# A written issue order for VectorE, ScalarE and GpSimd in the first 13 units of a fused attention, gated-FFN and FFT kernel

## The chip, the cores and the metric

The kernel runs on one core of a Trainium2 chip. The metric is device time in microseconds: the median of three runs. Besides, one execution was profiled; its span is the time from the first to the last instruction of the program.

## What is computed

Three layers in a row, all in float32, over 4 batches of 576 tokens (32 global, 512 local) and 512 features (8 heads of 64):

```python
# 1 attention: local tokens see a band of +-32 keys and the global ones; global tokens see all
s_l = concatenate([scale*q_l@k_g.T, where(|i-j|<=32, scale*q_l@k_l.T, -1e9)])
out = concatenate([sm(scale*q_g@k_all.T)@v_all, sm(s_l)@v_all])      # sm: e/(sum(e)+1e-9)
# 2 gated feed-forward with a convolution over tokens, d_ff = 1024
h = relu(x @ w_in)
c = conv_w[0]*h[t-1] + conv_w[1]*h[t] + conv_w[2]*h[t+1]
x = (h * sigmoid(c)) @ w_out
# 3 FFT mixing, layer norm and a feed-forward of 2048
u = x + real(fft(fft(x, tokens), features))
y = u + relu(norm(u) @ w_ch1) @ w_ch2
```

The weights arrive as 64-bit floats and are turned into float32 on the chip.

## The kernel before, in words

**Units.** The attention is cut into 32 units (`NU`; batch, half of the local tokens, pair of heads). For unit i, `load_qk` brings queries and keys, `s_mm` (called S below) makes four 128x224 score tiles on TensorE, `s_max` (M, L311) adds the mask and takes the row maximum on VectorE, `s_exp` (E, L323) does the exponentials on ScalarE, `s_norm` (L328 to L334) adds 1e-9 and inverts the sums on VectorE and scales the four tiles on GpSimd, `t_mm` (T) transposes them on TensorE, `t_evac` (L353) copies them out (VectorE one half, ScalarE the other), and `pv_mm` (V) multiplies by the values. `pv_evac` (L389, L390) splits the result into a high and a low part. The last two units of a half batch also run the global tokens (`sg_piece`, `pg_soft`, `pg_trans`, `pg_pv`).

**Feed-forward.** Layer 2 runs in 64 pieces u, two per unit from unit 6 on: `m_g1` (F, 12 matmuls and the ReLU, L479), `m_conv` (L489 to L491), `m_tanh` (L497), `m_gate` (L508 to L510) and three pieces later `m_g2` (D, 12 matmuls). Every operand of a matmul is a high and a low part (`mm3`: three products).

**Weights.** Layer 2 has 16 weight tiles of 128x512. For each, `fetch_w` loads 512 KB, and `make_w` makes the two float32 parts: absolute value on ScalarE (L167), clamp on GpSimd (L168), the low word's shift (ScalarE L170 for even tiles, VectorE L172 for odd ones), two joins of bits on VectorE (L174, L175), a copy to the high part on ScalarE (L203), and the low part on VectorE (L204). Two buffers `mag` hold the values in between. The list `wsteps` places the 16 in the program's units 0 to 8. Twelve of layer 3's tiles go the same way in units 11, 13, ..., 33 (`KEEP0`, `keep_make`), and are stored to DRAM for later.

**Order.** On SP (which issues the loads) and TensorE the instructions stand in the order in which the program writes them. On VectorE, ScalarE and GpSimd a list scheduler orders them, with a priority for each function (`PRIORITY`). On the chip each engine takes its instructions strictly in its order, each one waiting for its semaphores. After the attention come the FFT by matmuls, the layer norm and the last feed-forward, some 480 us of mostly TensorE work.

Of the kernel before, what the change touches and what calls it, by code (L numbers as in the profile page):

```python
# [38 lines left out]
MT = [(0, 92), (92, 92), (184, 90)]  # L39

# [88 lines left out]
def fused_kernel(ctx: ExitStack, tc: tile.TileContext, d, out):  # L129
# [172 lines left out]

    @prio("ev")
    def s_max(i):
        sb = s_bank.pop(i)
        sm = ap2.tile([128, 16], F32, tag="sm", name="sm", bufs=4)
        smalls[i] = sm
        for h in range(2):
            for a in range(2):
                k = 2 * h + a  # L310
                dve.tensor_tensor_reduce(  # L311
                    out=pbs(i)[h][:, a, 0:224], in0=sb[h][:, a], in1=mask[:, 2 * where(i)[1] + a], scale=-0.125,
                    scalar=3.0e38, op0=ALU.add, op1=ALU.min, accum_out=sm[:, k:k + 1],
                )
# [69 lines left out]
    def pv_evac(w):  # L384
        b, half, pp = where(2 * w)
        pvb = pv_bank.pop(w).rearrange("p (a q) -> p a q", a=2)
        t0 = SG + 256 * half
# [4 lines left out]
    smg_t = {}

    @prio("glo")
    def sg_piece(g, piece, tag):
# [5 lines left out]
        if piece == 0:  # L401
            smg_t[g] = ap2.tile([128, 8], F32, tag="smg", name="smg")
        sm = smg_t[g]
        with pri("ev"):
            dve.tensor_tensor_reduce(
                out=sg4s[g % 2][:, kc], in0=sb, in1=gmask[:, kc], scale=-0.125, scalar=3.0e38, op0=ALU.add,
                op1=ALU.min, accum_out=sm[:, piece:piece + 1],
            )
# [12 lines left out]

    @prio("glo")
    def pg_trans(g, tag, tag2):
        p = ap1.tile([128, 5, 128], F32, tag="pgt", name="pgt")
        t1, t2 = bank(tag), bank(tag2)
# [4 lines left out]
        with pri("ev"):  # L430
            act.copy(p[:, 0:4], t1.rearrange("p (s c) -> p s c", s=4))
            dve.tensor_copy(p[:, 4], t2[:, 0:128])
        pg_t[g] = p

    @prio("glo")
    def pg_pv(g, tag):
        b, gg = divmod(g, 2)
# [8 lines left out]
        xh, xl = get_xt(b)  # L446
        cs = slice(2 * gg, 2 * gg + 2)
        with pri("ev"):
            act.copy(xh[:, cs, 0:SG], o)
            dve.tensor_sub(xl[:, cs, 0:SG], o, f32(xh[:, cs, 0:SG]))  # L450
# [16 lines left out]
    def m_g1(u, tag):  # L467
# [10 lines left out]
        with pri("ev"):  # L478
            act.activation(hbuf[u % NHB][:, h0:h0 + n], o, AF.Relu, scale=0.5)  # L479

    @prio("me")
# [500 lines left out]
```

## Time and profile before

| | us |
|---|---|
| median of 3 runs (lowest, highest) | 799.74 (797.51, 800.78) |
| the profiled execution | 796.53 |
| its span | 794.6 |
| busy in the span: TensorE / VectorE / ScalarE / GpSimd | 765.2 / 477.9 / 365.1 / 159.2 |

The profiled execution is 3.2 us faster than the median of the runs; 1.9 us of its time lie outside its span. Busy time of TensorE counts a matmul at half the clock for twice as long, and a wait inside a group of matmuls can hide in it. In the rows of the views, a time in front of an instruction is its start from the beginning of the span, then comes its duration; brackets give the idle time of the engine before it and what ended it.

### The profile page before, as it was taken

The page shows a single profiled execution, that of the slowest core. Times are in us where ns is not written, and L with a number is a line of the kernel's source. Part 1 is how long each engine was busy: PE and PEld are TensorE (multiplying, and loading weights), DVE is VectorE, ACT ScalarE, POOL GpSimd, SP SyncE. Part 2 cuts the span into 40 slices and gives each one's busy share as a digit, 9 for nine tenths or more (in the row PEclk, how much of TensorE's full clock was granted, in tenths as well). Part 3 has the DMA queues.
Part 4 walks back from the last instruction along what each step waited for, and adds up shares of the span by engine and source line. Part 5 has one row for each costly group of instructions (what it writes and reads, how often), then busy time and mean ns, then how long its engine had stood idle before and what let it go on. Part 6 is the DMA issues. An engine that isn't in the chain of part 4 may idle for free.

```text
span 794.6 us, 13609 instructions
## 1 busy us (share of the span) xinstructions
PE 765.2 (96%) x5272; PEld 704.4 (89%) x5272; DVE 477.9 (60%) x1167; ACT 365.1 (46%) x884; POOL 159.2 (20%) x213
## 2 busy tenths in 40 slices
PE   6589999999999999999999999999999999999997
PEld 4368989998999988899889999999999999999997
DVE  6999787778777877699775778535422232213113
ACT  6787776777677775545533384313122112211110
POOL 5644423222322221000222022100022012100000
PEclk9889999999999999999999999999999999999999
DMA  8913423442345233436530670020200020001001
GB/s 310 401 45 108 141 79 126 135 168 79 127 134 169 78 111 107 115 114 234 182 102 1 225 254 1 1 91 0 66 26 2 1 90 1 1 1 45 1 1 45
DMA packets 36944, 77.80 MB, mean 98 GB/s; under 512 B 3768, under 2 KB 22072, under 8 KB 36880
## 3 DMA queue, kind: packets, MB, share of 16 engines
q1 hardware_dynamic: 36288, 74.52, 27.0%
q0 software_dynamic: 592, 2.42, 1.2%
q8 instruction: 41, 0.67, 0.3%
q14 instruction: 23, 0.19, 0.1%
HBM read 61.72 MB, written 15.20 MB: 97 GB/s over the span
## 4 chain that ended last, share of the span: by engine, by line
PE 85%; DVE 7%; DMA 3%; ACT 3%; issue 1%; POOL 1%; SPq 0%; DVEq 0%; POOLq 0%; ACTq 0%
PE ps_a L146 34%; PE ps_g L146 23%; PE ps_pv L146 15%; PE ps_s L146 6%; PE ps_t L146 3%; DMA qk<-in_qk_dram 2%; PE ps_s L344 1%; PE ps_t L344 1%; PE ps_s L345 1%; PE ps_t L345 1%; DMA uc<-u_d 1%; ACT pb L323 1%; DVE uc L857 1%; DVE cf L854 1%; DVE mag L174 1%
## 5 line engine op out<-in xcount | busy, mean ns | idle before, releaser
L146 PE MATMUL ps_a<-g,w_w 128*128 128x254 f32 (+1 forms) x768 | 112.7, 295 | 0.2 <-DVE u L541 0.2
L146 PE MATMUL ps_g<-x,w_w 128*128 128x256 f32 (+1 forms) x768 | 111.0, 293 | 1.1 <-ACT h L479 1.1
L146 PEld LDWEIGHTS ps_g<-x,w_w 128*128 128x128 f32 x768 | 100.3, 188 | 6.6 <-issue 4.4
L146 PEld LDWEIGHTS ps_a<-g,w_w 128*128 128x128 f32 x768 | 100.8, 190 | 4.5 <-issue 3.8
L146 PE MATMUL ps_a<-hd,w_w 128*128 128x436 f32 (+1 forms) x480 | 101.4, 360 | 0.0
L334 POOL TENSOR_SCALAR pb<-pb,sm 128x224 f32<-128x224 f32 x128 | 76.1, 613 | 109.2 <-DVE sm L329 42.3
L146 PEld LDWEIGHTS ps_a<-hd,w_w 128*128 128x128 f32 x480 | 90.1, 188 | 4.8
L826 DVE SCALAR_TENSOR_TENSOR hd<-ps_g,hd 128x436 fp32r<-128x436 f32 (+1 forms) x40 | 24.3, 608 | 88.7 <-ACT hd L825 88.7
L168 POOL TENSOR_SCALAR mag<-mag 128x512 f32<-128x512 f32 x48 | 39.6, 827 | 185.0 <-ACT mag L167 183.6
L146 PE MATMUL ps_a<-hd,w_v 128*128 128x436 f32 (+1 forms) x360 | 76.2, 360 | 0.0
L826 DVE SCALAR_TENSOR_TENSOR hd<-ps_pv,hd 128x436 fp32r<-128x436 f32 (+1 forms) x40 | 24.2, 605 | 85.1 <-ACT hd L825 85.1
L825 ACT ACTIVATE hd<-ps_pv 128x436 fp32r<-128x436 f32 (+1 forms) x40 | 21.3, 533 | 115.0 <-PE ps_pv L146 115.0
L825 ACT ACTIVATE hd<-ps_g 128x436 fp32r<-128x436 f32 (+1 forms) x40 | 21.3, 534 | 110.1 <-PE ps_g L146 110.0
L146 PEld LDWEIGHTS ps_a<-hd,w_v 128*128 128x128 f32 x360 | 67.6, 188 | 3.7
L323 ACT ACTIVATE pb<-pb,sm 128x224 f32<-128x224 f32 x128 | 60.4, 473 | 10.6 <-DVE sm L311 10.3
L490 DVE SCALAR_TENSOR_TENSOR y<-h,convw,y 128x254 f32<-128x254 f32 (+1 forms) x64 | 33.7, 527 | 29.0 <-ACT y L489 29.0
L146 PE MATMUL ps_g<-chl,w_w 128*128 128x436 f32 (+1 forms) x240 | 51.0, 361 | 0.0
L146 PE MATMUL ps_s<-qk 64*128 64x224 f32 (+1 forms) x144 | 38.3, 418 | 13.1 <-DMA qk<-in_qk_dram 8.0
L146 PE MATMUL ps_pv<-chl,w_v 128*128 128x436 f32 (+1 forms) x240 | 50.8, 360 | 0.0
L146 PE MATMUL ps_pv<-chl,w_w 128*128 128x436 f32 (+1 forms) x240 | 50.8, 360 | 0.0
L146 PEld LDWEIGHTS ps_pv<-chl,w_v 128*128 128x128 f32 x240 | 45.1, 188 | 2.5
L146 PEld LDWEIGHTS ps_g<-chl,w_w 128*128 128x128 f32 x240 | 44.8, 188 | 2.7 <-issue 0.3
(221 smaller groups left out, 1422.5 us busy)
## 6 DMA issues: line engine op xcount, KB each, us to landing
v<-in_v_dram SPq DMA_DIRECT2D x16, 640.0 KB, 4.9
qk<-in_qk_dram SPq DMA_DIRECT2D x16, 464.0 KB, 5.3
raw_r<-in_ch_dram SPq DMA_DIRECT2D x14, 512.0 KB, 6.2
raw_v<-in_ch_dram SPq DMA_DIRECT2D x13, 512.0 KB, 9.4
kept<-w_o SPq DMA_DIRECT2D x12, 512.0 KB, 3.8
w_w<-kept SPq DMA_DIRECT2D x12, 512.0 KB, 4.4
qk<-in_qk_dram SPq DMA_DIRECT2D x16, 304.0 KB, 4.9
u_d<-u SPq DMA_DIRECT2D x4, 1088.0 KB, 5.2
```

Source lines behind the costliest of these rows:

```text
L146: return pe.matmul(o, a, b, start=start, stop=stop)
L168: (clamp or dve).tensor_scalar(mag, mag, TOP, 2.0, op0=ALU.min, op1=ALU.max)
L174: dve.scalar_tensor_tensor(val, val, 3, tail, op0=ALU.logical_shift_left, op1=ALU.bitwise_or)
L323: last_exp[0] = act.activation(p, p, AF.Exp, bias=sm[:, k:k + 1], scale=-1.0, accum_out=sm[:, 4 + k:5 + k])
L334: gp.tensor_scalar(p, p, sm[:, k:k + 1], 1.0, op0=ALU.mult, op1=ALU.mult)
L344: pe.transpose(tb[:, 128 * a:128 * a + 128], pb[:, a, 0:128], ident)
L345: pe.transpose(tb[:, 256 + 128 * a:384 + 128 * a], pb[:, a, 128:256], ident)
L490: dve.scalar_tensor_tensor(y, hb[:, cc - 1:cc - 1 + n], convw2[:, m, 0:1], y, op0=ALU.mult, op1=ALU.add)
L825: act.activation(hd[:, 0], o, AF.Relu)
L826: dve.scalar_tensor_tensor(hd[:, 1], o, 0.0, f32(hd[:, 0]), op0=ALU.max, op1=ALU.subtract)
L854: dve.tensor_mul(tmp[:, e], acc[e], rs_t[c])
L857: dve.tensor_add(o, o, tmp[:, e])
```

## The change

The first 13 units (0 to 12) are no longer written as a loop. A table `PLAN` lists their steps one by one, each named by a short code and its indices, and inside it the order of VectorE, ScalarE and GpSimd is the written one too, not the scheduler's. The functions are split so that the table can place each instruction: `M3.0` is the first mask-and-maximum of unit 3, `E3.0` its exponential, `A3` and `R3` the sum plus 1e-9 and its inverse, `N3.0` a scaling, `T3.0` and `C3.0` transpose and copy-out, `XH`, `XL` the split of an attention result, `F5` and `D5.0` the feed-forward matmuls, `Y`, `TH`, `B` convolution, tanh and gate. `lw4` loads the fourth weight tile, and `wa wc wt/wu ws wo wh wl` are its seven steps (`wt` the shift on ScalarE, `wu` on VectorE). From unit 13 on the loop runs as before.

Besides the order: `A` runs on ScalarE where VectorE had L328 (13 times, and twice `GA` where it had L416); 10 of 16 shifts are `wt` on ScalarE where 8 were; four `mag` buffers instead of two (two of them borrowed from the tile that `keep_make` uses later); the table places the loads, and weight 0 is loaded second of all; the keep tiles start at unit 15 and come at 15, 16, 18, 20, 21, ..., 33; `pg_pv` of the first global piece uses bank `pv` instead of `a3`. TensorE's order is the same but for that bank.

```diff
+AHEAD = 13
-KEEP0 = 11
+KEEP0 = 15
+PLAN = """
+lg lq0 lw0 lm1 lq1 li lv0 lw1 S0 lm0 lq2 lc lq3 wu0 wa0 lv1 M0.0 wc0 M0.1 E0.0 M0.2 E0.1 M0.3 S1 ws0 E0.2 E0.3 wo0 A0 lw2 R0 M1.0 wh0 N0.0 lw3 M1.1
...
-    keep_at = {KEEP0 + 2 * k: x for k, x in enumerate(KEPT)}
+    keep_at = {KEEP0 + 5 * k // 3: x for k, x in enumerate(KEPT)}
...
+    def s_add(i):
+        sm = smalls[i]
+        act.activation(sm[:, 8:12], sm[:, 4:8], AF.Copy, bias=1e-9)
+
+    def s_recip(i):
+        sm = smalls[i]
+        dve.reciprocal(sm[:, 12:16], sm[:, 8:12])
...
+    def micro():
+        pair = rb.tile([128, 2, 512], F32R, tag="o", name="mag2")
+        ring = [f32(pair[:, k]) for k in range(2)] + [mp.tile([128, 512], F32, tag="mag", name="mag", bufs=2) for _ in range(2)]
...
+        def w_clamp(k):
+            mag = word(k)[0]
+            gp.tensor_scalar(mag, mag, TOP, 2.0, op0=ALU.min, op1=ALU.max)
...
+        def w_join(k):
+            mag, _, tail = word(k)
+            val = bits(mag)
+            dve.scalar_tensor_tensor(val, val, 3, tail, op0=ALU.logical_shift_left, op1=ALU.bitwise_or)
...
     with tc.manual_schedule(engines={mybir.EngineType.SP, mybir.EngineType.PE}):
-        load_qk(0)
-        sp.dma_start(mask[:, 2:4], d["mask"][:, 2:4])
-        load_qk(1)
-        sp.dma_start(ident, d["ident"])
-        load_qk(2)
...
-        wsteps = [0, 1, 2, 4, 6, 8, 10, 12, 14, 16]
...
-        for i in range(NU + 2):
+        others = {mybir.EngineType.Activation, mybir.EngineType.DVE, mybir.EngineType.Pool}
+        with tc.manual_schedule(engines=others):
+            ops = micro()
+            for x in PLAN:
+                name, *at = re.findall(r"[A-Za-z]+|\d+", x)
+                ops[name](*map(int, at or [0]))
+        for i in range(AHEAD, NU + 2):
...
-            if i < 9:
-                with tc.issue_after(last_exp[0].ins):
-                    for k in range(wsteps[i], wsteps[i + 1]):
-                        make_w(wq[k])
```

How it moves instructions, at three places. First SP, the first loads of the program, before (`raw_w` is a weight tile, `v` the values, `qk` queries and keys):

```order
L273 DMA qk<-in_qk_dram 128x608
L545 DMA mask<-in_mask_dram 128x448
L273 DMA qk<-in_qk_dram 128x608
L547 DMA ident<-in_ident_dram 128x128
L273 DMA qk<-in_qk_dram 128x608
L182 DMA raw_w_135<-in_w_in_dram 128x4x256
L280 DMA v<-in_v_dram 128x1280
```

and in the change:

```order
L296 DMA qk<-in_qk_dram 128x608
L205 DMA raw_w_129<-in_w_in_dram 128x4x256
L698 DMA mask<-in_mask_dram 128x448
L296 DMA qk<-in_qk_dram 128x608
L699 DMA ident<-in_ident_dram 128x128
L303 DMA v<-in_v_dram 128x1280
L205 DMA raw_w_137<-in_w_in_dram 128x4x256
```

The first weight tile now stands ahead of the mask that M of unit 0 reads and of the second `qk`.

Second VectorE, from unit 0 to the first row of unit 1, before:

```order
L557 MEMSET eps 128x1
L311 ISA pb_90,sm<-ps_s,mask 128x224
...
L311 ISA pb_91,sm<-ps_t,mask 128x224
L311 ISA sm 128x1
L328 TENSOR_SCALAR sm<-sm 128x4
L329 RECIPROCAL sm<-sm 128x4
L311 ISA pb_92,sm<-ps_a_166,mask 128x224
```

and in the change:

```order
L755 MEMSET eps 128x1
L656 TENSOR_SCALAR raw_w_129<-raw_w_129 128x512
L336 ISA pb_90,sm<-ps_s,mask 128x224
...
L336 ISA pb_91,sm<-ps_t,mask 128x224
L336 ISA sm 128x1
L661 SCALAR_TENSOR_TENSOR mag_121<-mag_121,raw_w_129 128x512
L666 SCALAR_TENSOR_TENSOR mag_121<-raw_w_129,mag_121 128x512
L354 RECIPROCAL sm<-sm 128x4
L336 ISA pb_92,sm<-ps_a_163,mask 128x224
```

A shift of weight 0 now stands ahead of the first M, the addition L328 is gone from this engine, and two joins stand where it stood.

Third VectorE, the rows just ahead of unit 9's first M, before:

```order
L329 RECIPROCAL sm<-sm 128x4
L204 TENSOR_TENSOR w_w_757<-mag,w_w_757 128x512
L490 SCALAR_TENSOR_TENSOR y<-h_96,convw_61,y 128x254
L204 TENSOR_TENSOR w_w_766<-mag,w_w_766 128x512
L432 COPY pgt<-ps_t 128x128
L491 SCALAR_TENSOR_TENSOR y<-h_96,convw_61,y 128x254
L490 SCALAR_TENSOR_TENSOR y<-h_97,convw_61,y 128x254
L491 SCALAR_TENSOR_TENSOR y<-h_97,convw_61,y 128x254
L508 SCALAR_TENSOR_TENSOR y<-y,h_96 128x254
L311 ISA pb_90,sm<-ps_s,mask 128x224
```

and in the change:

```order
L678 TENSOR_TENSOR w_w_822<-mag_121,w_w_822 128x512
L492 COPY pgt<-ps_t 128x128
L578 SCALAR_TENSOR_TENSOR y<-y,h_98 128x254
L666 SCALAR_TENSOR_TENSOR mag<-raw_w_699,mag 128x512
L661 SCALAR_TENSOR_TENSOR mag<-mag,raw_w_702 128x512
L583 TENSOR_TENSOR g<-y,g 128x254
L666 SCALAR_TENSOR_TENSOR mag<-raw_w_702,mag 128x512
L336 ISA pb_90,sm<-ps_s,mask 128x224
```

Before, 14 weight tiles are finished (L204) ahead of unit 9's row; in the change 10 (L678). In all, ahead of that row there are fewer: 2 of L174, 2 of L175, 4 of L204, 4 of L490 and L491 together, 3 of L172, 9 of L328, 2 of L416 and 1 of L508. Ahead of the first row of unit 13, fewer: 2 of L172, 13 of L328, 2 of L416, 1 of L490 or L491, and one keep tile (one each of L174, L175, L204).

## Rows read from the trace of the kernel before

**Rows 1.** The page: busy tenths in 40 slices of the span (19.9 us each).

```profile
PE   6589999999999999999999999999999999999997
...
DVE  6999787778777877699775778535422232213113
```

**Rows 2.** Waits of TensorE in the whole span: us in total, times, longest.

```profile
PE ps_s L146 <- DMA qk<-in_qk_dram: 8.0, 2, 4.3
PE ps_s L146 <- DVE smg L405: 5.1, 2, 4.3
```

**Rows 3.** Windows of the span: busy us of each engine, granted clock, DMA share, GB/s.

```profile
5.58:73.37 67.79, 51.63 (x410) 39.63 (x411) 62.81 (x191) 54.00 (x147) 40.96 (x54) 0.90 0.64 236
73.37:110.77 37.40, 37.40 (x356) 34.77 (x354) 31.33 (x94) 27.16 (x79) 11.34 (x18) 1.00 0.34 116
110.77:317.00 206.23, 205.07 (x1911) 187.36 (x1912) 157.79 (x491) 147.32 (x414) 54.77 (x95) 1.00 0.36 119
```

**Rows 4.** Timeline of VectorE: the first rows of units 0, 9 and 13.

```profile
5.58 0.39 DVE L311 CUSTOM_DVE_ANT_0 pb<-ps_s,mask 128x224 f32<-128x224 f32 x1 [3.98 <-PE ps_t L146]
...
5.89 0.39 DVE L311 CUSTOM_DVE_ANT_0 pb<-ps_s,mask 128x224 f32<-128x224 f32 x1
...
73.36 0.38 DVE L311 CUSTOM_DVE_ANT_0 pb<-ps_s,mask 128x224 f32<-128x224 f32 x1
...
110.77 0.39 DVE L311 CUSTOM_DVE_ANT_0 pb<-ps_s,mask 128x224 f32<-128x224 f32 x1 [0.23 <-PE ps_t L146]
```

**Rows 5.** VectorE's groups in 0 to 100 us: count, busy us, mean ns, idle before.

```profile
L175 DVE SCALAR_TENSOR_TENSOR mag<-raw_w,mag 128x512 int32<-128x512 int32 x16 | 11.6, 723 | 0.1
L174 DVE SCALAR_TENSOR_TENSOR mag<-mag,raw_w 128x512 int32<-128x512 int32 x16 | 11.2, 701 | 0.4 <-POOL mag L168 0.4
L204 DVE TENSOR_TENSOR w_w<-mag,w_w 128x512 fp32r<-128x512 f32 x16 | 11.1, 696 | 0.2
...
L490 DVE SCALAR_TENSOR_TENSOR y<-h,convw,y 128x254 f32<-128x254 f32 x8 | 4.8, 606 | 0.2 <-ACT y L489 0.2
...
L491 DVE SCALAR_TENSOR_TENSOR y<-h,convw,y 128x254 f32<-128x254 f32 x8 | 4.4, 544 | 0.1
L508 DVE SCALAR_TENSOR_TENSOR y<-y,h 128x254 f32<-128x254 f32 x8 | 4.0, 503 | 0.6 <-ACT y L497 0.5
L172 DVE TENSOR_SCALAR raw_w<-raw_w 128x512 int32<-128x512 int32 x8 | 3.9, 485 | 0.0
...
L328 DVE TENSOR_SCALAR sm<-sm 128x4 f32<-128x4 f32 x12 | 1.9, 162 | 3.4 <-ACT pb L323 3.4
```

**Rows 6.** Timeline, units 0 and 1: the second qk load, its wait, the first weight load.

```profile
1.66 0.42 SPq L273 DMA_DIRECT2D qk<-in_qk_dram  x1
...
5.61 0.38 SPq L182 DMA_DIRECT2D raw_w<-in_w_in_dram  x1
...
6.34 1.86 PE L146 MATMUL ps_a<-qk 64*128 64x224 f32 x8 [0.80 <-DMA qk<-in_qk_dram]
...
8.99 0.68 ACT L167 ACTIVATE mag<-raw_w 128x512 f32<-128x512 f32 x1 [1.01 <-DMA raw_w<-in_w_in_dram]
```

**Rows 7.** ScalarE's groups in 0 to 100 us, columns as in rows 5.

```profile
L167 ACT ACTIVATE mag<-raw_w 128x512 f32<-128x512 f32 x16 | 10.8, 673 | 7.5 <-DVE w_w L204 5.7 <-DMA raw_w<-in_w_in_dram 1.8
L203 ACT CAST w_w<-mag 128x512 fp32r<-128x512 f32 x16 | 9.8, 614 | 4.9 <-DVE mag L175 4.7
...
L497 ACT ACTIVATE y<-y 128x254 f32<-128x254 f32 x8 | 3.3, 414 | 2.7 <-DVE y L491 2.7
...
L449 ACT CAST x<-ps_a 128x64 fp32r<-128x64 f32 x1 | 0.2, 204 | 0.0
```

**Rows 8.** DMA issues: count, KB each, median us from issue to landing.

```profile
raw_w<-in_w_in_dram SPq DMA_DIRECT2D x8, 512.0 KB, 9.7
```

**Rows 9.** Timeline of VectorE: one instruction (L508) twice.

```profile
55.87 0.41 DVE L508 SCALAR_TENSOR_TENSOR y<-y,h 128x254 f32<-128x254 f32 x1
...
72.62 0.82 DVE L508 SCALAR_TENSOR_TENSOR y<-y,h 128x254 f32<-128x254 f32 x1
```

More of the change, by code (lines that the diff above doesn't have):

```diff
@@ L301, in pbs, with pb_of, s_max @@
         return [pbuf[2 * (i % NPB) + h] for h in range(2)]
+    def pb_of(i, k):
+        return pbs(i)[k // 2][:, k % 2, 0:224]
     @prio("ev")
[L304 to L314, printed above, removed]
+    def s_max(i, ks=range(4)):
+        sb = s_bank[i]
+        if i not in smalls:
+            smalls[i] = ap2.tile([128, 16], F32, tag="sm", name="sm", bufs=4)
+        sm = smalls[i]
+        for k in ks:
+            dve.tensor_tensor_reduce(
+                out=pb_of(i, k), in0=sb[k // 2][:, k % 2], in1=mask[:, 2 * where(i)[1] + k % 2], scale=-0.125,
+                scalar=3.0e38, op0=ALU.add, op1=ALU.min, accum_out=sm[:, k:k + 1],
+            )
@@ L429, in pg_trans, with pg_evac @@
         pe.transpose(t2[:, 0:128], sg4[:, 512:640], ident)
-        with pri("ev"):
+    @prio("ev")
+    def pg_evac(g, parts=range(2)):
+        if g not in pg_t:
+            pg_t[g] = ap1.tile([128, 5, 128], F32, tag="pgt", name="pgt")
+        p, (t1, t2) = pg_t[g], pg_bank[g]
+        if 0 in parts:
             act.copy(p[:, 0:4], t1.rearrange("p (s c) -> p s c", s=4))
+        if 1 in parts:
             dve.tensor_copy(p[:, 4], t2[:, 0:128])
-        pg_t[g] = p
+    pgv_bank = {}
     @prio("glo")
@@ L445, in pg_pv, with pgv_evac @@
                     mm(o[64 * h:64 * h + 64, c], v[r, t, 64 * n:64 * n + 64], p[r, t, SG * n:SG * n + SG], t == 0, t == 4)
[L446 to L450, printed above, removed]
+    @prio("ev")
+    def pgv_evac(g, parts=range(2)):
+        b, gg = divmod(g, 2)
+        o = pgv_bank[g]
+        xh, xl = [x[:, 2 * gg:2 * gg + 2, 0:SG] for x in get_xt(b)]
+        if 0 in parts:
+            act.copy(xh, o)
+        if 1 in parts:
+            dve.tensor_sub(xl, o, f32(xh))
     w_raw, w_in, w_out = {}, {}, {}
@@ L499, in m_gate @@
     @prio("me")
-    def m_gate(u):
+    def m_gate(u, parts=range(3)):
         if not 0 <= u < NM:
@@ L532, in m_g2 @@
         if part == 1:
[L533 to L548 removed]
+            del gate[u]
@@ new lines, in m_g2, with m_sum @@
+        if evac and kt == 7:
+            m_sum(u, part)
+    @prio("ev")
+    def m_sum(u, part, parts=range(3)):
+        b, half = u // 16, 1 - (u // 8) % 2
+        o0, n = TOK[half][0:2]
+        if half == 1 and part == 0 and 0 in parts:
+            eo_tile(b)
+        o = eo_t[b][:, :, o0:o0 + n]
+        if 0 in parts:
+            act.copy(o[:, part + 2], acc[part + 2])
+        if 1 in parts:
+            dve.tensor_add(o[:, part], acc[part], o[:, part + 2])
+        if 2 in parts:
+            dve.tensor_sub(o[:, part + 2], acc[part], o[:, part + 2])
```

331 lines of the change are left out of this document (222 added, 109 removed).

## The prediction

> **What bounds the kernel now.** I read the slices of the page first. TensorE is at 9 tenths from the fifth slice to the last but one; only the first four slices (80 us) and the last show less [rows 1]. The change touches units 0 to 12, so the question is how early TensorE becomes full. In the same first slices VectorE is at 6 to 9 tenths. The waits of TensorE name only a part of what it loses: 8.0 us for two loads of `qk` and 5.1 us for `smg` on VectorE [rows 2]; the rest hides inside groups of matmuls, so I go by windows instead. I cut the span where VectorE starts the mask-and-maximum M of units 0, 9 and 13: at 5.58, 73.36 and 110.77 us [rows 4]. In the first window VectorE is busy 62.81 of 67.79 us, 92.7%; TensorE 51.63, a part of it at half clock (mean granted 0.90), ScalarE 54.00 and GpSimd 40.96 [rows 3]. **VectorE is the bound there.** In the second window TensorE is busy all 37.40 us and VectorE 31.33, so TensorE is the bound; after that, up to 317 us, TensorE is busy 205.07 of 206.23 [rows 3]. So a microsecond saved ahead of unit 13 should last to the end, as long as TensorE stays full behind it.
>
> **The change, part by part.** An instruction of VectorE holds the engine 0.08 us less than its listed time: of unit 0, rows that start at 5.58 and 5.89 last 0.39 each [rows 4]. I take mean minus 0.08.
>
> *Work taken from in front of unit 9's M.* The two orders differ there by the counts under the third place of the order. With the means of [rows 5]: 2 joins L174 at 0.62 are 1.24; 2 joins L175 at 0.64, 1.28; 4 low parts L204 at 0.62, 2.48; 4 convolution taps at 0.50 (the middle of 0.606 and 0.544, less 0.08), 2.00; 3 shifts L172 at 0.41, 1.23; 9 additions L328 at 0.08, 0.72; 2 of L416 (one column) at the same, 0.16; 1 gate L508 at 0.42. Sum 9.5 us. VectorE's work between the two M falls from 62.81 to 53.3 us. At the busy share of before, 92.7%, that takes 57.5 us instead of 67.8.
>
> *First loads.* Weight 0 (512 KB) now goes ahead of the mask that the first M needs, and VectorE's very first row, the shift of weight 0, waits for it too. Before, the third load was issued at 1.66 and its wait ended at 6.34 [rows 6], with 304, 112 and 304 KB queued up to it; now the mask is third and 304, 512 and 112 KB are queued up to it. From below this costs nothing (the mask before was in time for 5.58); from above, 208 KB more than what had landed at 6.34, at the same 720 KB in 5.6 us (from 0.74), is 1.6 us, so it lands at 7.9, 2.3 late. I take 0.8, nearer to the lower end, since the rate of that stretch holds the start-up of the first transfer. The Trainium skill, SBUF — State Buffer, section The DMA setup-cost knee, gives a transfer about 2 us plus its bytes at 436 GB/s. By that, an estimate, the 928 KB land about 4.2 us after the first issue, and the cost is nothing; no run here shows it yet. First M at 6.4, then; unit 9's M at 6.4 + 57.5 = 63.9, against 73.36: **9.5 us earlier.**
>
> *Between unit 9 and unit 13.* What was taken away comes back here, less what is gone for good ahead of unit 13: 2 shifts at 0.41, 15 additions at 0.08, one tap at 0.5, and one keep tile (0.62 + 0.64 + 0.62 = 1.88), in all 4.4 us. VectorE has 31.33 + 9.5 − 4.4 = 36.4 us of work in a stretch in which TensorE needs 37.40. Both are nearly full. At least it takes 37.4 us; at VectorE's share of before, 36.4 / 0.927 = 39.3. I take the second, since the VectorE of the first window shows how much it idles when others feed it: **1.9 us given back.**
>
> *ScalarE.* Ahead of unit 9's exponentials it loses 2 L167 at 0.67, 3 L203 at 0.61 and four of the feed-forward's rows at L497's 0.41, and gains a shift of L167's size and 11 small additions at the time of the 128x64 row L449, 0.20 [rows 7]: 54.0 − 1.3 − 1.8 − 1.6 + 0.7 + 2.2, some 52 us in 57.5. It is hidden, but its cover is thin (some 90% busy); I cost it at nothing in the sum and put it into a rival.
>
> *Four `mag` buffers* end waits of ScalarE, 5.7 us for the low part that frees a buffer [rows 7], which is off the bound; nothing. *GpSimd* keeps its rows; nothing. *SP*: the loads of `qk` now stand ahead of most weights, which ends TensorE's 8.0 us of waits for them [rows 2]; these are inside the 67.8 us and not counted again, since VectorE was busy meanwhile. *Keep tiles* from unit 15 on: 12 instead of 11 in the units from 13 on, 1.9 us on VectorE, which is busy 157.79 of 206.23 us [rows 3]: covered. *One bank* for the first global piece: its TensorE group then waits for the split of unit 5's result, with other matmuls ahead; nothing.
>
> **Sum**: 9.5 − 1.9 = 7.6 us. Against the profiled execution, 796.5 − 7.6 = 788.9; this execution was 3.2 us below the median of the runs, so the median should be 799.7 − 7.6 = **792.1 us**.
>
> **The rivals.**
>
> *A. VectorE's waits go as well.* Four buffers and other work between dependent steps may fill its 5.0 us of idle time. For it: the addition L328 alone waits 3.4 us for exponentials [rows 5], and in the change two joins stand in that place. Against: most of it lies in the first units, where TensorE and ScalarE have nothing to give. In full: M of unit 9 at 6.4 + 53.3 = 59.7, then 37.4: 13.7 earlier, 786.0. Half of it: 789.
>
> *B. Waits in place of work.* Three engines in fixed orders each wait in front of the row that is late, and ScalarE and VectorE are both above 90% busy. If VectorE reaches only 87%, unit 9 is at 6.4 + 61.3 = 67.7 (5.7 earlier) and the next stretch takes 41.8 (4.4 longer): 1.3 us gained, 798.4. So VectorE's share decides: at 85% nothing is left. Against: before, too, the order on the chip was fixed.
>
> *C. GpSimd in the way.* The same gate instruction L508 takes 0.41 us once and 0.82 another time [rows 9], and its mean of 0.503 lies between. The mechanism would be that closer packing makes GpSimd's scalings meet VectorE's rows more often. If the 36 taps and gates and the 48 weight rows ahead of unit 13 grew by 0.07 us each, a sixth of the way from the short to the long one, 5.9 us would go and 1.7 be left: 798.0. The Trainium skill, SBUF — State Buffer, section Who interferes with whom, says that a VectorE instruction with two SBUF inputs and a GpSimd instruction that reads SBUF block each other for a whole instruction. By that rule, the long L508 agrees, though the trace does not show what held it. Against: GpSimd's 41 us lie in some 58 instead of 68 us, which is a sixth more meetings, not more than that.
>
> *D. Slower: weights that are just too late.* SP issues in order, and a load of values that waits for TensorE stands ahead of later weights. A weight took 3.4 us to ScalarE's first use with little else in the queue (5.61 to 8.99, [rows 6]) and 9.7 us in the median [rows 8]. In the written order, weights 8 and 10 to 12 stand some 4 to 6 us of VectorE's rows ahead of their first use. Should each come in 9.7, about 4.5 us late, VectorE's M queue behind them: 4 x 4.5 = 18 us, 10 slower than before, 810. It turns to slower once such stalls pass 7.6 + 4 us. Against: 16 weights now spread over 60 us, so the queue is mostly empty.
>
> **How the numbers follow.** Forecast 0.55 (789.5 to 795), A 0.20, B and C together 0.17, D 0.08. A measurement of this kernel can tell 0.5%, 4.0 us, from no change. Faster by more than that (below 795.7) is the forecast nearly whole, A, and a fifth of B and C: 0.78. Slower (above 803.7) is D: 0.08. The rest, 0.14, is within. The range, 786.0 to 798.2, takes in A and half of B and C, and both ends of the first loads (792.1 − 0.8, + 1.5).
>
> **What would show it.** M of unit 9 near 64 us and of unit 13 near 103 us in the profile after; VectorE busy over 90% from 7 to 100 us; TensorE without `qk` waits, full from about 62 us; the window from unit 13 on as long as before. If M of unit 9 comes after 68 us, the sum is wrong at VectorE's share; if it is early and unit 13 is not, at the second stretch; if the gain of unit 13 is lost before the end, at TensorE staying full.

## The result, and the profile after

The changed kernel takes 791.25 us (median of 4 runs, 790.32 to 792.18) against 798.77 us (4 runs, one more than at the outset, 797.51 to 800.78): a ratio of 0.9903, 95% interval 0.9877 to 0.9930. Run again (experiment 5) it gave 790.98 us, ratio 0.991 (0.9884 to 0.9936). Its profiled execution took 790.96 us with a span of 789.2 us.

The windows between the first mask rows M of units 0, 9 and 13, cut in the profile after as in [rows 3] (busy us of TensorE, weight loads, VectorE, ScalarE, GpSimd, then granted clock, DMA share, GB/s), and VectorE's timeline at their edges:

```profile
6.47:63.81 57.34, 47.48 (x424) 36.78 (x425) 53.55 (x163) 51.38 (x150) 34.81 (x51) 1.00 0.71 263
63.81:103.42 39.61, 37.03 (x341) 33.59 (x341) 36.73 (x100) 29.79 (x88) 15.54 (x21) 1.00 0.24 84
```

```profile
6.47 0.39 DVE L336 CUSTOM_DVE_ANT_0 pb<-ps_s,mask 128x224 f32<-128x224 f32 x1 [1.00 <-DMA mask<-in_mask_dram]
...
63.81 0.38 DVE L336 CUSTOM_DVE_ANT_0 pb<-ps_s,mask 128x224 f32<-128x224 f32 x1
...
103.42 0.39 DVE L336 CUSTOM_DVE_ANT_0 pb<-ps_s,mask 128x224 f32<-128x224 f32 x1
```

Unit 0 starts 0.9 us later than before, unit 9 comes 9.6 us earlier (63.81 against 73.36) and unit 13 7.35 us earlier (103.42 against 110.77). VectorE is busy 93.4% of the first window (92.7% before) and 92.7% of the second (83.8% before); TensorE is no longer full in the second, 37.03 of 39.61 us. From unit 13 to the end of the span this execution takes 685.8 us, the one before took 683.8. So of the 7.35 us about 2 do not reach the end in this pair of executions, and 1.5 of them go behind the attention's last mask row (491.7 us from there to the end before, 493.2 after), far behind the table's units. The medians differ by 7.5. From unit 13 on it lasted 683.8 to 686.8 us in the twelve experiments; what makes it longer or shorter is open.

The waits of VectorE up to unit 9 in the profile after (us in total, times, longest):

```profile
DVE sm L354 <- ACT sm L350: 1.0, 2, 0.8
DVE pb L336 <- DMA mask<-in_mask_dram: 1.0, 1, 1.0
DVE g L583 <- ACT g L581: 0.8, 1, 0.8
```

and those of TensorE that answer to [rows 2]:

```profile
PE ps_s L169 <- DMA qk<-in_qk_dram: 3.7, 1, 3.7
PE ps_a L376 <- POOL pb L359: 1.7, 3, 1.0
...
PE ps_a L169 <- DMA qk<-in_qk_dram: 1.6, 1, 1.6
PE ps_s L169 <- DVE smg L440: 1.5, 2, 1.1
```

The wait for the sums is down to 1.0 us in this window; before, L328 waited 2.3 us for exponentials up to unit 9, and 3.4 us in the first 100 us [rows 5]. Of TensorE's 8.0 us of waits for `qk` ahead of bank `s` [rows 2], 3.7 are left.

### The profile page after: what moved, and what is told of

Same layout as the page of the kernel before. It is cut to its first block, busy times and chain, and to the rows that moved or that the text cites. A ratio compares the mean times of both kernels' runs of the same rounds, so it can differ in the third digit from the quotient of the medians.

```text
span 789.2 us, 13595 instructions
## 1 busy us (share of the span) xinstructions
PE 761.0 (96%) x5272; PEld 700.3 (89%) x5272; DVE 477.9 (61%) x1150; ACT 366.5 (46%) x901; POOL 159.6 (20%) x213
## 4 chain that ended last, share of the span: by engine, by line
PE 70%; DVE 14%; ACT 9%; DMA 4%; issue 2%; SPq 0%; POOL 0%; ACTq 0%; DVEq 0%; POOLq 0%
PE ps_a L169 29%; PE ps_g L169 19%; PE ps_pv L169 14%; PE ps_s L169 4%; ACT pb L346 3%; PE ps_t L169 3%; DVE y L563 3%; DMA raw_w<-in_w_out_dram 2%; DVE g L583 1%; DMA uc<-u_d 1%; DVE pb L336 1%; DVE mag L661 1%; DVE mag L197 1%; ACT y L559 1%; DVE mag L198 1%
## 5 line engine op out<-in xcount | busy, mean ns | idle before, releaser
L359 POOL TENSOR_SCALAR pb<-pb,sm 128x224 f32<-128x224 f32 x128 | 78.8, 632 | 105.3 <-DVE sm L354 67.1
L563 DVE SCALAR_TENSOR_TENSOR y<-h,convw,y 128x254 f32<-128x254 f32 (+1 forms) x128 | 69.0, 540 | 23.3 <-ACT y L559 22.5
L1009 DVE SCALAR_TENSOR_TENSOR hd<-ps_g,hd 128x436 fp32r<-128x436 f32 (+1 forms) x40 | 24.3, 609 | 88.7 <-ACT hd L1008 88.7
L1008 ACT ACTIVATE hd<-ps_g 128x436 fp32r<-128x436 f32 (+1 forms) x40 | 21.3, 533 | 110.4 <-PE ps_g L169 110.3
L346 ACT ACTIVATE pb<-pb,sm 128x224 f32<-128x224 f32 x128 | 60.4, 473 | 10.3 <-DVE sm L336 10.2
L191 POOL TENSOR_SCALAR mag<-mag 128x512 f32<-128x512 f32 x32 | 25.9, 810 | 185.6 <-ACT mag L190 185.1
L169 PEld LDWEIGHTS ps_pv<-chl,w_w 128*128 128x128 f32 x240 | 44.9, 188 | 2.5
```

The costliest lines, as they stand in the source:

```text
L169: return pe.matmul(o, a, b, start=start, stop=stop)
L191: (clamp or dve).tensor_scalar(mag, mag, TOP, 2.0, op0=ALU.min, op1=ALU.max)
L359: gp.tensor_scalar(pb_of(i, k), pb_of(i, k), sm[:, 12 + k:13 + k], 1.0, op0=ALU.mult, op1=ALU.mult)
L563: dve.scalar_tensor_tensor(y, o, convw2[:, m, x:x + 1], y, op0=ALU.mult, op1=ALU.add)
L1008: act.activation(hd[:, 0], o, AF.Relu)
L1009: dve.scalar_tensor_tensor(hd[:, 1], o, 0.0, f32(hd[:, 0]), op0=ALU.max, op1=ALU.subtract)
```

## The experiments

The time of each kernel stands beside that of the kernel before on the same chip: 797.9 us for the first four, 798.5 for the next four, 797.5 for the last four. The theory at the outset was the prediction's: VectorE's work ahead of a unit, divided by a busy share of some 93%, sets when that unit comes. The rivals were that the written order saves waits (not work), that ScalarE is as much the bound, and that the loads matter. In each row of a window the granted clock is the third figure from the end: it differs from run to run, and VectorE's share has to be read beside it (the last section).

### 1. Work added to VectorE: `e1_more_vector`

```diff
 def s_add(i):
-    act.activation(sm[:, 8:12], sm[:, 4:8], AF.Copy, bias=1e-9)
+    dve.tensor_scalar(sm[:, 8:12], sm[:, 4:8], 1e-9, None, op0=ALU.add)
...
-            "wt": w_tail,
+            "wt": w_shift,
```

(and `pg_add` in the same way)

> The changed kernel, with the 15 small additions and all 16 shifts of the weights on VectorE. Theory (VectorE's work divided by the share of time it is busy, about 93%, sets units 0 to 12): ahead of unit 9's first mask row there are 5 more shifts at 0.41 us and 11 to 15 more additions at 0.08, in all 4.6 * 0.62-free rows summed to 3 to 4.6 us more, so that row comes at 67 to 69 us instead of 63.8; ahead of unit 13's 10 shifts and 15 additions, 5.3 us more, 5.7 later at the same share, at about 109 instead of 103.4; the time is 797 instead of 791.3. Rival (the gain lies in waits that the written order and the four magnitude buffers removed): VectorE's added rows fill its idle time, unit 13 less than 2 us later, the time below 793.5.

Measured: 795.71 us, ratio 0.9965 (0.9951 to 0.9979), so 4.7 us more than the change's 790.98. Its profile is of the fastest of its ten executions, 792.41 us:

```profile
6.63:66.51 59.88, 48.97 (x425) 38.00 (x426) 58.25 (x183) 45.80 (x130) 35.47 (x52) 0.97 0.69 254
66.51:106.78 40.27, 37.01 (x340) 33.49 (x340) 37.69 (x105) 28.62 (x83) 15.26 (x21) 1.00 0.24 82
```

VectorE's work up to unit 9 grew by 4.7 us, 53.55 to 58.25, but unit 9 came only 2.7 later, because VectorE was now busy 97.3% of the window. Unit 13 came 3.4 us later, at 106.78. The share is no constant; that VectorE waits less because 5.6 us were taken from ScalarE is argued, not shown. The cost in the median lies near the theory's (5.7), but the mechanism in the profile is not the one it names, and the other nine executions have no profile.

### 2. Work taken from VectorE: `e2_less_vector`

```diff
-            "wu": w_shift,
+            "wu": w_tail,
```

> The changed kernel, with all 16 shifts on ScalarE. VectorE loses 6 shifts of 0.41 us (5 ahead of unit 9, 2.0 us; 2.5 us ahead of unit 13). Theory (VectorE alone is the bound): unit 9's first mask row 2.1 us earlier, at 61.7, unit 13's 2.6 earlier, at 100.8, time 788.7. Rival (ScalarE is as much the bound, since it is busy 51.4 of the 57.3 us to unit 9): 5 shifts of 0.57 us more on it make 54.2 of 55; unit 9 not earlier or later than 63.8, time 791 or more.

Measured: 793.81 us (0.9945, 0.9925 to 0.9964), slower than the change by 2.8 us. The profile:

```profile
6.17:66.81 60.64, 49.99 (x423) 38.78 (x424) 51.70 (x158) 53.76 (x154) 33.88 (x52) 0.94 0.68 249
```

VectorE has 1.9 us less to do and unit 9 comes 3.0 us later; VectorE is busy 85.3%. A part of the 3.0 us belongs to a stretch in which TensorE ran at a granted clock of 0.5 (mean 0.94 in this window). The change's second profile (experiment 5) has the same clock in this window: against it the window is 1.8 us longer with 1.9 us less to do, and the share 85.3% instead of 91.1%. So the rival holds there: ScalarE, busy 53.76 us, is as much the bound. The time at like clock differs less than the medians: the executions at 0.999 or 1.0 over the span took 791.3 to 792.2 us here (three) and 789.1 to 791.0 in the change (four), about 1 us apart.

### 3. The same program with the scheduler's order: `e3_scheduler`

```diff
-        with tc.manual_schedule(engines=others):
+        with nullcontext():
             ops = micro()
```

> The changed kernel's program, same steps in the same written sequence, same loads, buffers and placement, but VectorE, ScalarE and GpSimd ordered by the scheduler within it as in the kernel before. Its order puts 2.1 us more VectorE work ahead of unit 9's first mask row (10 finished weight tiles, as in the change) and 0.5 us more ahead of unit 13's. Theory (the amount of work ahead decides, at 93% busy): unit 9 at about 66.1, unit 13 at about 104, time about 792. Rival (the written order itself saves waits): VectorE's busy share to unit 9 falls below 90%, unit 13 after 107, time above 795.

Measured: 796.56 us (0.9986, 0.9972 to 1.0): of the change's gain 1.4 us are left. Units 9 and 13 come at 68.3 and 112.4:

```profile
7.13:68.33 61.20, 51.09 (x418) 38.51 (x419) 55.66 (x168) 52.94 (x154) 34.44 (x51) 0.94 0.66 241
68.33:112.45 44.12, 40.69 (x347) 37.86 (x347) 34.87 (x97) 29.00 (x86) 12.78 (x18) 0.88 0.22 76
```

Steps, loads, buffers and placement are worth little with the scheduler's order. Up to unit 9 VectorE's share is 90.9%, no less than in the change's second profile at the same clock (91.1% at 0.94, experiment 5): the 3.2 us by which unit 9 comes later than there are 2.1 us more work and a start 0.8 us later. So the rival's sign for this window, a share below 90%, did not come. Behind unit 9 the share falls to 79.0%; there TensorE once waits 3.4 us for the high part of a weight, and it runs at half clock from 73.9 to 84.1 us. The rival holds in the second window alone, and what the order and the clock each cost there is not separated.

### 4. The deferred weights alone: `e4_spread_weights`

```diff
-        wsteps = [0, 1, 2, 4, 6, 8, 10, 12, 14, 16]
+        wsteps = [0, 1, 2, 2, 3, 4, 5, 6, 8, 12, 14, 16]
...
-            if i < 9:
+            if i < 11:
```

> The kernel before, with one part of the change alone: the 16 weight tiles are placed later in its loop (over units 0 to 10 instead of 0 to 8; 9 instead of 14 finished ahead of unit 9's first mask row). Nothing else changes: two magnitude buffers, the old loads, the scheduler's order. By the order, 7.8 us of VectorE work move from ahead of unit 9 to behind it; ahead of unit 13 the work is the same. Theory: unit 9 at 5.6 + 55.0/0.927 = 64.9 instead of 73.4, then 39.1/0.927 = 42.2 us instead of 37.4, unit 13 at 107.1 instead of 110.8, time 3.7 below the kernel before, about 795. Rival (late weights make waits, or the gain of the change comes from its written order or its loads): unit 13 at 110 or later, time not below that of the kernel before by more than 1 us.

Measured: 808.5 us, ratio 1.0129 (1.011 to 1.0148): slower by 10.6 us. The windows, then waits of VectorE and of TensorE up to unit 13:

```profile
5.44:72.84 67.40, 51.29 (x410) 38.89 (x412) 54.35 (x178) 48.37 (x137) 31.67 (x49) 0.92 0.64 241
72.84:119.39 46.55, 40.04 (x355) 36.05 (x352) 39.82 (x106) 32.49 (x89) 15.43 (x22) 0.96 0.28 94
```

```profile
DVE sm L328 <- ACT pb L323: 6.1, 7, 2.2
...
DVE y L490 <- ACT y L489: 3.5, 2, 1.9
```

```profile
PE ps_g L146 <- DVE w_w L204: 4.5, 2, 3.6
PE ps_g L146 <- ACT h L479: 4.0, 3, 2.1
```

VectorE's work ahead of unit 9 fell by 8.5 us, from 62.81 to 54.35 (7.8 were counted); unit 9 came at 72.8, hardly earlier than before. Nearly all that was taken away turned into waits (busy 80.6%); the longest, for exponentials of ScalarE, grew from 2.3 to 5.0 us up to unit 9. Behind unit 9 the work came back in full, and TensorE waited 4.5 us for low parts of weights. Taking work from in front of a unit gave nothing here by itself. But this is not the change's placement (9 instead of 10 tiles are finished ahead of unit 9, with two `mag` buffers): with that placement experiment 3 lost nothing, so the 10.6 us are not the price of deferring as such.

### 5. The change again: `e5_after_again`

No edit; it stands as the mark for the next three.

> The changed kernel once more, unchanged, on the chip of the next three, so that they have it beside them: 791.3, as its four runs gave, and M of unit 9 near 63.8.

Measured: 790.98 us. Unit 9 came at 65.1 in its profile, unit 13 at 104.7, each 1.3 us later than in the first profile, with the same rows in the same order; the last section says why. Up to unit 9 VectorE was busy 91.1%:

```profile
6.31:65.13 58.82, 50.66 (x424) 39.97 (x425) 53.57 (x163) 51.56 (x150) 34.79 (x52) 0.94 0.70 257
```

### 6. Mask and second qk first: `e6_mask_first`

```diff
-lg lq0 lw0 lm1 lq1 li lv0 lw1 S0 lm0 lq2 lc lq3 wu0 wa0 lv1 M0.0 wc0 M0.1 E0.0 M0.2 E0.1 M0.3 S1 ws0
+lg lq0 lm1 lq1 lw0 li lv0 lw1 S0 lm0 lq2 lc lq3 lv1 M0.0 M0.1 E0.0 M0.2 E0.1 M0.3 wu0 wa0 wc0 S1 ws0
```

> The changed kernel with one step of its loads undone: the mask and the second qk are issued ahead of weight 0, and the first shift of weight 0 stands behind unit 0's mask rows on VectorE. Theory (the first loads cost the 0.9 us by which unit 0 starts later than before, and VectorE's work behind it decides): unit 0 at 5.6 instead of 6.5, units 9 and 13 0.9 earlier, time 790.4. Rival (the weight that is late instead holds the units behind it): unit 1 or 2 not earlier, unit 9 at 63.8 or later, time 791.3 or more.

Weight 0's absolute value on ScalarE and its clamp (`wa0`, `wc0`) move back too. Measured: 794.05 us (0.9949, 0.9928 to 0.9969), 3.1 slower than the change. The timeline of VectorE shows unit 0 early and unit 1 late:

```profile
5.60 0.39 DVE L336 CUSTOM_DVE_ANT_0 pb<-ps_s,mask 128x224 f32<-128x224 f32 x1 [4.01 <-PE ps_t L169]
...
8.21 0.43 DVE L656 TENSOR_SCALAR raw_w<-raw_w 128x512 int32<-128x512 int32 x1 [1.28 <-DMA raw_w<-in_w_in_dram]
9.64 0.69 DVE L661 SCALAR_TENSOR_TENSOR mag<-mag,raw_w 128x512 int32<-128x512 int32 x1 [1.00 <-POOL mag L648]
10.37 0.69 DVE L666 SCALAR_TENSOR_TENSOR mag<-raw_w,mag 128x512 int32<-128x512 int32 x1
10.98 0.17 DVE L354 RECIPROCAL sm<-sm 128x4 f32<-128x4 f32 x1
11.06 0.36 DVE L336 CUSTOM_DVE_ANT_0 pb<-ps_a,mask 128x224 f32<-128x224 f32 x1
```

Weight 0 lands 1.28 us after VectorE wants it and its joins stand in front of unit 0's inverse L354, so everything behind waits for a weight that nobody needs yet: unit 1 at 11.1 instead of 9.2, unit 9 at 65.6. The rival holds. In a written order a row that is late by its load is late for all rows behind it.

### 7 and 8. One engine alone in the written order: `e7_vector_written`, `e8_scalar_written`

```diff
-        others = {mybir.EngineType.Activation, mybir.EngineType.DVE, mybir.EngineType.Pool}
+        others = {mybir.EngineType.DVE}
```

and, in the second, `{mybir.EngineType.Activation}`.

> The changed kernel with VectorE alone in the written order in units 0 to 12, ScalarE and GpSimd ordered by the scheduler. VectorE's rows stand exactly as in the change. Theory 1 (VectorE's order, with the deferred weights, is what counts): unit 9 within 1 us of 63.8, time below 792.5. Theory 2 (what feeds VectorE counts as much: ScalarE's order, which is busy 90% of the time to unit 9): VectorE's busy share to unit 9 below 91%, unit 13 at 105 or later, time above 793.

> The changed kernel with ScalarE alone in the written order, VectorE and GpSimd ordered by the scheduler, which puts about the same weight rows ahead of unit 9 as the change (10 finished) but 4 instead of 3 us more of them between units 9 and 10. Theory 1 (VectorE's own written order counts): the loss of the scheduler's order stays, time above 795. Theory 2 (ScalarE's order is the half that was wrong with the scheduler): time below 793, VectorE's busy share to unit 9 at 92% or more.

Measured: 804.15 us (1.0073, 1.0051 to 1.0095) and 800.96 us (1.0029, 1.0016 to 1.0043). Either half of the written order alone is slower than none of it (796.6) and slower than the kernel before. For VectorE alone, the window to unit 9, then VectorE and ScalarE around 31 us:

```profile
6.15:72.15 66.00, 51.92 (x408) 38.27 (x410) 53.32 (x163) 51.89 (x152) 34.30 (x52) 0.94 0.62 231
```

```profile
27.46 0.68 DVE L661 SCALAR_TENSOR_TENSOR mag<-mag,raw_w 128x512 int32<-128x512 int32 x1
31.18 0.18 DVE L354 RECIPROCAL sm<-sm 128x4 f32<-128x4 f32 x1 [3.04 <-ACT sm L350]
```

```profile
28.31 0.67 ACT L644 ACTIVATE mag<-raw_w 128x512 f32<-128x512 f32 x1 [1.34 <-DMA raw_w<-in_w_out_dram]
...
29.80 0.68 ACT L644 ACTIVATE mag<-raw_w 128x512 f32<-128x512 f32 x1
30.38 0.68 ACT L652 ACTIVATE raw_w<-raw_w 128x512 int32<-128x512 uint32 x1
30.96 0.19 ACT L350 ACTIVATE sm<-sm 128x4 f32<-128x4 f32 x1
```

VectorE has exactly the change's rows in the change's order, 53.32 us of work up to unit 9, and takes 66.0 us for them (80.8%) instead of 57.3, or 58.8 in the change's second profile, whose clock is the same 0.94. One step of the loss is in the rows: the scheduler put weight rows on ScalarE, one of them waiting for its load, ahead of the small addition L350, and VectorE's next row is the inverse that needs it: 3.04 us idle, 10.1 us for such waits up to 70 us. For ScalarE alone VectorE's share to unit 9 is 82.6% (51.99 of 62.95 us). Theory 1 of the first and theory 2 of the second both fall: neither order is the good one by itself. That it is the fit of the two is what experiment 10 tests.

### 9. The loads alone: `e9_loads_later`

```diff
-                while fetched < min(16, (2, 4, 7, 10, 13, 16)[min(i, 5)]):
+                while fetched < min(16, 2 * i + 1):
```

(in the kernel before)

> The kernel before with its weight loads alone moved: two per unit instead of three from unit 2 on, so that the loads of qk stand ahead of more weights. Placement of the weights, buffers and the scheduler stay; the scheduler's order then has 12 finished weight tiles ahead of unit 9's first mask row instead of 14, 2.2 us less VectorE work. Theory (the loads are a side matter; VectorE is fed or not by the orders of VectorE and ScalarE): TensorE's 8 us of waits for qk fall, unit 9 at 71 to 73.5, time 796.5 to 798.5. Rival (the qk that came late was what held the first units, and the change's gain is its load order): unit 9 at 66 or earlier, time below 794.

Measured: 796.77 us (0.9981, 0.997 to 0.9992), 0.7 us less than before. Unit 9 came at 71.5 and unit 13 at 110.4, VectorE busy 91.2% up to unit 9. As the theory had it, though TensorE's waits for `qk` fell from the 8.0 us of [rows 2] to 3.9 us, about as in the change: moving these loads is a side matter. (The change moves the first ones otherwise; experiments 6 and 12 bear on those.) VectorE had 2.6 us less work up to unit 9, and unit 9 came 1.8 us earlier, so here taking work away did help; at unit 13 0.3 us of it were left.

### 10. VectorE and ScalarE written, GpSimd scheduled: `e10_vector_scalar`

```diff
-        others = {mybir.EngineType.Activation, mybir.EngineType.DVE, mybir.EngineType.Pool}
+        others = {mybir.EngineType.Activation, mybir.EngineType.DVE}
```

> The changed kernel with VectorE and ScalarE both in the written order, GpSimd alone ordered by the scheduler. With either engine alone written the time was 804.2 and 801.0. Theory (the two orders have to fit each other; GpSimd, busy 61% of the time, follows): VectorE's busy share to unit 9 at 91% or more, unit 13 at 103 to 105.5, time 790.5 to 792.5. Rival (it takes all three): time above 795.

Measured: 793.43 us (0.9942, 0.9919 to 0.9965). Unit 13 came at 106.8, VectorE's share to unit 9 was 88.7%; unit 0 itself started at 7.1. Both expectations miss: two of the three written orders give 4.1 us where the change gave 7.5 on the chip of experiment 5 (it was not run on this one), and GpSimd's, busy 57% of this window, seems to be worth the rest. Behind unit 9 nothing is lost: up to unit 13 it took 39.63 us, as in the change. The two intervals overlap a little, the clock up to unit 9 was 0.97, and unit 0's start differs between executions of the same first loads (see the point on them below), so the size of that rest is not settled.

| in the written order | time, us | ratio to before | interval |
|---|---|---|---|
| none (3) | 796.56 | 0.9986 | 0.9972 to 1.0 |
| VectorE (7) | 804.15 | 1.0073 | 1.0051 to 1.0095 |
| ScalarE (8) | 800.96 | 1.0029 | 1.0016 to 1.0043 |
| VectorE, ScalarE (10) | 793.43 | 0.9942 | 0.9919 to 0.9965 |
| all three (5) | 790.98 | 0.991 | 0.9884 to 0.9936 |

### 11. Low parts on GpSimd: `e11_low_gpsimd`

```diff
-            dve.tensor_sub(w[:, 1], ring[k % 4], f32(w[:, 0]))
+            (gp if k > 9 else dve).tensor_sub(w[:, 1], ring[k % 4], f32(w[:, 0]))
```

> The changed kernel with the low parts of the last 6 weight tiles (k = 10 to 15) on GpSimd instead of VectorE, at the same places of the written order. Most of them stand behind unit 9, where VectorE was busy 36.7 of 39.6 us and GpSimd 15.5. Theory (VectorE's work sets the stretch from unit 9 to 13, down to TensorE's 37.4): 3.7 us less VectorE work, the stretch takes 37.4 to 38 us, time 1.5 to 2.2 lower, 789. Rival (the fit of the orders decides, and GpSimd's scalings now stand behind the low parts, which wait for ScalarE): the stretch takes 39.6 or more, time 791 or more.

Measured: 796.37 us (0.9982, 0.997 to 0.9994), 5.4 slower than the change. The window from unit 9 to 13, and three groups in it:

```profile
66.23:108.11 41.88, 37.05 (x344) 33.76 (x346) 36.78 (x96) 29.96 (x88) 19.94 (x26) 1.00 0.23 79
```

```profile
L666 DVE SCALAR_TENSOR_TENSOR mag<-raw_w,mag 128x512 int32<-128x512 int32 x5 | 4.8, 951 | 0.1
...
L583 DVE TENSOR_TENSOR g<-y,g 128x254 fp32r<-128x254 f32 x5 | 3.5, 693 | 0.2 <-ACT g L581 0.2
...
L678 POOL TENSOR_TENSOR w_w<-mag,w_w 128x512 fp32r<-128x512 f32 x6 | 8.0, 1334 | 4.7 <-ACT w_w L673 4.7
```

In the change the same two groups of VectorE are:

```profile
L666 DVE SCALAR_TENSOR_TENSOR mag<-raw_w,mag 128x512 int32<-128x512 int32 x5 | 3.8, 757 | 0.0
...
L583 DVE TENSOR_TENSOR g<-y,g 128x254 fp32r<-128x254 f32 x5 | 2.3, 465 | 0.0
```

Six subtractions, 4.3 us on VectorE, went away, and VectorE was still busy 36.78 us in this window (36.73 in the change): its other rows grew longer, among them L578 from 417 to 693 ns. Timeline of GpSimd, then of VectorE, for two of the six:

```profile
70.25 1.26 POOL L678 TENSOR_TENSOR w_w<-mag,w_w 128x512 fp32r<-128x512 f32 x1 [4.50 <-ACT w_w L673]
...
83.93 1.29 POOL L678 TENSOR_TENSOR w_w<-mag,w_w 128x512 fp32r<-128x512 f32 x1 [0.17 <-ACT w_w L673]
```

```profile
70.53 1.28 DVE L578 SCALAR_TENSOR_TENSOR y<-y,h 128x254 f32<-128x254 f32 x1 [0.51 <-ACT y L568]
...
84.19 1.31 DVE L583 TENSOR_TENSOR g<-y,g 128x254 fp32r<-128x254 f32 x1 [0.15 <-ACT g L581]
```

Each of the six meets one such row of VectorE, and that row ends only 0.3 to 0.6 us after the subtraction: five take 0.83 to 1.31 us where L578 and L583 elsewhere in this window take 0.41 to 0.50, and the sixth, an L666 at 64.53, just ahead of unit 9, takes 1.77. Besides, a low part takes 1.33 us on GpSimd instead of 0.71, and TensorE waited 3.3 us for two of them. So the theory was not tested cleanly; what the run shows is that lending these rows to GpSimd, at these places, did not pay. Of the 4.7 us by which unit 13 came later (108.11), 2.3 lie in this window; the rest lies ahead of it, where the granted clock was 0.94. The Trainium skill, SBUF — State Buffer, section Who interferes with whom, says that a VectorE instruction with two SBUF inputs and a GpSimd one that reads SBUF hold each other up; L666, L578 and L583 have two, and the run agrees: the six rows above outlast the subtractions that they meet.

### 12. The mask one place earlier: `e12_mask_second`

```diff
-lg lq0 lw0 lm1 lq1 li lv0 lw1 S0 lm0 lq2 lc lq3 wu0 wa0 lv1 M0.0 wc0 M0.1 E0.0 M0.2 E0.1 M0.3 S1 ws0
+lg lq0 lm1 lw0 lq1 li lv0 lw1 S0 lm0 lq2 lc lq3 wa0 lv1 M0.0 wc0 M0.1 E0.0 M0.2 E0.1 M0.3 wu0 S1 ws0
```

> The changed kernel with the mask issued just ahead of weight 0 (the second qk stays behind it), and weight 0's shift behind unit 0's mask rows. Theory: unit 0's mask row at 5.6 instead of 6.4, weight 0 later by 112 KB, 0.3 us; unit 1 not later than 9.2; the later units within 0.5 us of the change, time 790 to 791.5. Rival (as where the mask and the second qk went ahead: the joins of weight 0 that stand ahead of unit 0's inverse wait for it): unit 1 at 10 or later, time above 793.

Measured: 792.02 us (0.993, 0.9902 to 0.9957), within the spread of the change. Neither expectation held whole: unit 1 was late as the rival had it, the time was not. Unit 0 started at 5.5, but unit 1 at 10.3, and unit 13 0.8 us later than in the change: ScalarE's first row is weight 0's absolute value, which waited to 7.42 for its load, and unit 0's exponentials stand behind it. The saving at the start is lost in the same way as in experiment 6.

No variant was faster than the change. A ring of two buffers in the written order was not tried: the table takes up a weight before the one two places ahead is finished, so it would need another table. A written order with the weights where they stood before was not tried either.

## Why the prediction was right, point by point

The forecast was 792.1 us, in 786.0 to 798.2; measured 791.25. The steps, in their own numbers:

- **The work ahead of unit 9** was to fall from 62.81 to 53.3 us on VectorE: 53.55.
- **The first loads** were to cost 0.8 us (0 to 2.3): 0.9, unit 0 at 6.47, where VectorE waits 1.0 us for the mask. The estimate from the Trainium skill (SBUF — State Buffer, The DMA setup-cost knee), 4.2 us after the first issue, was too short: the wait for the mask ended at 6.47, 5.7 us after it. The measurement decides. It is one draw: in the eight other profiles with the same first loads unit 0 started at 5.83 to 7.13.
- **The busy share** was taken over from before, 92.7%: 93.4% (94.4% from 7 to 100 us). So unit 9 came at 63.81 (forecast 63.9). That it agrees so well is in part luck. The share of before belongs to a granted clock of 0.90, for which the sum had no term, and 93.4% to one of 1.00; in the second profile of the change, at 0.94, it was 91.1%, unit 9 came at 65.13 and unit 13 at 104.74.
- **The second stretch** was to take 39.3 us with 36.4 of VectorE's work: 39.61 with 36.73; unit 13 at 103.42 (forecast 103.2). TensorE was not "full from about 62 us", but it could not be with VectorE that full.
- **To the end**: 7.5 us in the medians, against 7.6; 5.6 in the two profiled executions. This too is in part luck. The window from unit 13 on was to be as long as before and was 2 us longer, so the profiled execution took 790.96 us, not the 788.9 of the sum; it lies 0.3 us below the median of its kernel, where the one before lay 2.2 below the median of four.
- **The `qk` waits** were to go: 3.7 of the 8.0 us [rows 2] are still there; they were not in the sum.

The sum came out, yet one step in it was not a step but a result: "At the busy share of before, 92.7%" was carried over as if it were VectorE's own. It is not. With nearly the same rows ahead of unit 9 it was 80.8% (VectorE alone written, granted clock 0.94 in that window), 82.6% (ScalarE alone, 0.92), 88.7% (both, 0.97), 90.9% (none, 0.94, and only 79.0% behind unit 9) and 93.4% (all three, 1.00; 91.1% at 0.94); with more of them 97.3% (0.97). Deferring the weights under the scheduler took 8.5 us of work away and gave nothing (experiment 4). So the cause, as far as these runs show it, has two halves: the table moves weight work behind unit 9 **and** places the rows of the three engines so that fewer of them stand in front of another's late row. The first without the second gained 1.4 us in experiment 3 and cost 10.6 in experiment 4; the second without the first was not run, and the clock was not held, so how the 7.5 us divide among order, placement and clock is open.

Of the rivals, *B*, waits in place of work, did not happen in the change but is what happens when VectorE's or ScalarE's order is taken out together with GpSimd's; the prediction gave it 0.17 together with C and argued against it only that "the order on the chip was fixed" before. By its own sum, 85% is 1.2 us slower than before; nothing is left at 86%. *C*, GpSimd in the way, was small in the change (53.55 us of work where 53.3 were forecast) and appeared in experiment 11. *A* did not come: VectorE's idle time fell from 5.0 to 3.8 us. *D*, weights just too late, did not come in the change (TensorE waited 1.2 us for one low part); in experiments 4, 6, 8 and 12 it did, by a row or two each. ScalarE, "hidden, but its cover is thin", was closer to a bound than the sum had it: 2.4 us more work on it, moved from VectorE, made the kernel 2.8 us slower, about 1 us at like clock.

## What to carry to other kernels

Summing the rows ahead of a point and dividing by the engine's busy share gives a good first number, but the share belongs to the whole set of orders: ask which engine's row each wait is for, and whether the change moves both sides of it together. When several engines near 90% feed each other, write their orders together or leave them all to the scheduler; one alone was worse than none here. In a written order put rows that depend on a load, or on a slow helper engine, behind the short links of the main chain (the sums and inverses here), not in front of them.

## What the runs showed of the hardware that was not expected

**The clock of TensorE moves a stretch that TensorE doesn't bound.** The change was profiled twice with the same rows in the same order. Both have nearly the same busy times in the 10 us before 32.3 us; then one ran at a granted clock of 0.5, the 1.2 GHz level, for 6.8 us, and the other at 1.00, 2.4 GHz. That stretch, first in the run of experiment 5, then in the first profile of the change:

```profile
32.30:39.10 6.80, 6.79 (x37) 5.86 (x38) 5.16 (x18) 5.53 (x18) 4.36 (x6) 0.50 0.95 353
```

```profile
32.30:39.10 6.80, 6.30 (x57) 5.32 (x57) 6.46 (x23) 6.77 (x20) 5.06 (x7) 1.00 0.98 358
```

At the lower level TensorE gets through 37 instructions instead of 57, and VectorE, which waits 1.6 us for TensorE there and not at all in the other, through 18 instead of 23. Unit 9 comes at 65.13 instead of 63.81, with 53.57 and 53.55 us of VectorE's work ahead. What TensorE did before:

```profile
22.00:32.30 10.30, 7.15 (x64) 4.66 (x64) 10.10 (x32) 9.13 (x28) 7.45 (x12) 1.00 0.78 282
```

```profile
22.00:32.30 10.30, 7.21 (x64) 4.73 (x64) 10.15 (x34) 9.19 (x28) 7.33 (x12) 1.00 0.77 282
```

It was busy about 70% in both (7.15 us where it fell, 7.21 where it did not), so these rows do not tell why one fell. The ten runs of experiment 2 point the same way: the three with a mean granted clock of 0.999 or 1.0 over the span took 791.3 to 792.2 us; of the seven others, at 0.993 to 0.996, one took 791.4 and six 793.6 to 797.5. The kernel before had two such stretches in its profile (granted 0.50 from 23.8 to 30.6 and from 40.8 to 47.7 us), so a part of the gain may be clock; no run here separates it.

The recorded executions give a size. The 57 of the kernel before that stand beside the experiments ran at a mean granted clock of 0.984 to 0.994 over the span, the change's eight at 0.996 to 1.0. Among the 57 a straight line falls by 2.7 us for each 0.01 of clock (median 798.6 us in the 22 up to 0.986, 797.5 in the 9 above 0.99); the change's eight took 790.3 us on average in the four at 1.0 and 791.9 in the other four. An estimate: should that line hold across the 0.011 between the means of the two kernels, some 3 of the 7.5 us go with the clock. It doesn't say which way: the falls may cost the time, or the waits that cost time may come with the falls.

**Two engines' rows stretch each other.** In experiment 11 VectorE's L583 went from 465 to 693 ns, L578 from 417 to 693 and L666 from 757 to 951 ns when six subtractions of GpSimd stood beside them: each subtraction met one row, which ended only after it. The work saved was lost in full.
